# V of batches 1 and 2 loaded in token rows, and k of batches 3 to 7 in token rows and transposed by DMA out of SBUF

## The chip, the cores and the metric

The kernel runs on one core of a Trainium2 chip. The metric is the device time of one execution in microseconds; the median of the runs of the kernel before is 349.85 us.

## The reference

Eight batches of eight heads attend over 576 tokens of 64 numbers each, every query to itself and the 63 keys before it. The heads' outputs of a token stand side by side as 512 numbers and go through two matrix products with `h - tanh(h)` between them.

```python
B, H, S, D = 8, 8, 576, 64                        # q, k, v: float32
scores = matmul(q, k.transpose(0, 1, 3, 2)) / sqrt(D)
rel = pos[:, None] - pos[None, :]
scores = where((rel >= 0) & (rel < 64), scores, -1e9)
attn = exp(scores - max); attn = attn / (sum(attn) + 1e-9)
x = matmul(attn, v).transpose(0, 2, 1, 3).reshape(B * S, H * D)   # 4608 x 512
h = x @ w_in                                      # 512 x 2048
return (h - tanh(h)) @ w_out                      # 2048 x 512
```

## The kernel before

**The attention** works on a pair of heads at a time. Pair `pr` of batch `b` is heads `pr` and `pr + 4`, and `g = 4 b + pr` counts the 32 pairs. The tokens are cut into nine windows of 64 queries. For window `j` the scores need the 128 keys from 64 before the window to its end; so `kT`, in which a column is a key and the 128 partitions are the two heads' 64 numbers, has 64 columns of zeros in front. `scores` (L256 to L264) multiplies three windows at a time with `qT` and lets ScalarE take the exponential. `masking` clears what lies outside the 64 keys, `pv` (L270) multiplies with V, `norm` divides by the sum, which a column of ones in V has produced, and writes `xs`. The outputs get to the feature-major tile `xT` through TensorE (`x_tr`, first batches) or through an SP DMA that transposes (`x_dma`, from batch 2 on).

**V** has to lie with 128 keys on the partitions for each of nine windows, and neighbouring windows share 64 keys: `vw[b % 2]`, 128 partitions by nine windows by eight heads by 65 (64 numbers and the one). There are two ways to fill it:

- Batches 0 to 2: V is loaded whole with eight tokens in a row of a partition (`load_v_all`, 72 partitions), cast into the tile `vb` pair by pair (`cast_v`), copied by nine DMAs into the upper halves of the windows (`keys_v`, L162), and the upper halves are copied to the next window's lower halves (`shift_v`: for batches 0 and 1 by VectorE, L168, for batch 2 by one SP DMA, L170).
- Batches 3 to 7: five POOL DMAs put 128 tokens each onto the partitions of every other window (`load_rows`, L175), in rows of 64 numbers that the DMA converts to bf16, and `cross_rows` (L181, L182) makes the halves that are still missing, with two VectorE copies.

**q and k** are loaded whole for a batch with six tokens in a partition's row (`load_all`, 96 partitions), cast by POOL pair by pair (`cast`, L85), and turned by six TensorE transposes a pair into PSUM (`tr`, L247), from which ScalarE and VectorE copy them into `qT` and `kT` (L83, L85). In batch 7 both are bounced through DRAM instead: `bounce` writes the cast rows out, and an SP DMA reads them back transposed (`tr_dma`, L138 and L141).

**The two matrix products** run over nine chunks of 512 tokens and 16 blocks of the 2048 hidden numbers: `hp_mm` (L317), the tanh on ScalarE (L321), the subtraction on VectorE (L327), and 16 steps later `yp_mm` (L337), `y_out` (L342) and the store on SP's queue (L344).

**The order** is written out by hand (`manual_schedule`). A loop counts half steps `h`; an even one issues the four matmuls of one block of the first product, an odd one four of the second. `items[h]` holds what else is issued at `h`. For the first twelve pairs that comes from the text `PLAN`, one token a call; what stands under -1 comes ahead of the first product. `V1` and `V2` are the loads of V of batches 1 and 2, `d..` casts, `k..` the copies to `vw`, `z..` the shifts, `K`, `Q` whole loads, `w0` to `w2` and `o0` to `o3` the weights. For pairs 12 to 31 a loop sets the places by formula: with `d` = 0, 2 or 4, the scores of pair `g` start at `a + 5`, `a = 8 g - 48 - d`, and loads are placed from the batch's mark `s = 32 b - d`. `pace` is a tiny POOL copy that reads a fresh hidden block, so that POOL doesn't issue a load too early:

```python
s = 32 * b - (0, 2, 4)[min(b - 3, 2)]
...
    for i in range(NF + 1):
        at(s - 59 + i, load_rows, b, i)
    at(s - 42, cross_rows, b)
...
        hq, hk = s - (60 if b < 7 else 68), s - (64 if b < 7 else 72)
```

Each engine takes its instructions in the order in which the loop issues them, so that one that waits holds what is behind it. Loads with conversion are issued by POOL, transposing DMAs and stores by SP.

Of the kernel before, what the change touches and what calls it, by code (L numbers as in the profile page):

```python
# [8 lines left out]
BF16 = mybir.dt.bfloat16  # L9
# [6 lines left out]
def kernel(  # L16
# [9 lines left out]
    nc = tc.nc  # L26
    B, H, S, D = q.shape
    NP = H // 2
    NJ = S // 64
    E, P = 6, S // 6  # L30
    EV, PV = 8, S // 8
# [40 lines left out]
    vb = const.tile([PV, EV, H, D + 1], BF16, name="vb")  # L72
    PT = [const.tile([128, NJ, 128], BF16, name=f"pt{i}") for i in range(NPT)]
    kT = [const.tile([128, 64 + S], BF16, name=f"kt{i}") for i in range(NR)]
    qT = [const.tile([128, 2, S], BF16, name=f"qt{i}") for i in range(NR)]
    qz = [const.tile([P, 2, E, 128], BF16, name=f"qz{i}") for i in range(2)]
    xs = [const.tile([128, NJ, NP, D], BF16, name=f"xs{i}") for i in range(2)]
# [9 lines left out]
    def load(g, n, eng):  # L87

        b, pr = divmod(g, NP)
        if eng is nc.gpsimd:  # L90
            if (b, n) not in whole:
                whole[b, n] = all_pool.tile([P, H, E * D], BF16, tag=n, name=n + "all")
            t = whole[b, n][:, pr::NP]
        else:
            t = qk_pool.tile([P, 2, E * D], F32, tag="f", name=n + "f")
        eng.dma_start(out=t, in_=(q if n == "q" else k)[b, pr::NP].rearrange("h (p e) d -> p h (e d)", e=E))
        stage[g, n] = t

    def load_all(b, n):

        t = all_pool.tile([P, H, E * D], BF16, tag=n, name=n + "all")
        nc.gpsimd.dma_start(out=t, in_=(q if n == "q" else k)[b].rearrange("h (p e) d -> p h (e d)", e=E))
        for pr in range(NP):
            stage[b * NP + pr, n] = t[:, pr::NP]
# [15 lines left out]
        for h in range(2):  # L120
            nc.gpsimd.tensor_copy(qz[g % 2][:, h, :, 64 * h:64 * h + 64], i[:, h])

    def bounce(g, n):

        if n == "q":
            t = dram.tile([2, S, 128], BF16, tag="q", name="qd")
            nc.sync.dma_start(out=t.rearrange("h (p e) c -> p h (e c)", e=E),
                              in_=qz[g % 2].rearrange("p h e c -> p h (e c)"))
        else:
            t = dram.tile([S, 128], BF16, tag="k", name="kd")  # L130
            nc.sync.dma_start(out=t.rearrange("(p e) c -> p (e c)", e=E),
                              in_=rows.pop((g, "k")).rearrange("p e h d -> p (e h d)"))
        rows[g, n + "d"] = t

    def tr_dma(g, n):
        t = rows.pop((g, n + "d"))
        if n == "q":
            nc.sync.dma_start(out=qT[g % NR].rearrange("c h s -> c (h s)"),  # L138
                              in_=t.rearrange("h s c -> (h s) c"), transpose=True)
        else:  # L140
            nc.sync.dma_start(out=kT[g % NR][:, 64:], in_=t, transpose=True)  # L141

    def load_v(b, pr):
        if (b, "v") not in whole:
# [1 line left out]
        t = whole[b, "v"][:, pr::NP]  # L146
        nc.gpsimd.dma_start(out=t, in_=v[b, pr::NP].rearrange("h (p e) d -> p h (e d)", e=EV))
        stage[b, pr, "v"] = t

    def load_v_all(b):  # L150
        t = v_pool.tile([PV, H, EV * D], BF16, tag="v", name="vall")
        nc.gpsimd.dma_start(out=t, in_=v[b].rearrange("h (p e) d -> p h (e d)", e=EV))
        for pr in range(NP):
            stage[b, pr, "v"] = t[:, pr::NP]

    def cast_v(b, pr, eng=nc.gpsimd):
        move(eng, vb[:, :, 2 * pr:2 * pr + 2, 0:D].rearrange("p e h d -> p h e d"),
# [4 lines left out]
        eng.dma_start(out=vw[b % 2][64:128, j].rearrange("p h c -> p (h c)"),  # L162
                      in_=vb[8 * j:8 * j + 8].rearrange("p e h c -> p e (h c)"))

    def shift_v(b, j0, j1, eng=nc.sync):
        lo, hi = vw[b % 2][0:64, j0 + 1:j1 + 1], vw[b % 2][64:128, j0:j1]
        if eng is nc.vector:
            eng.tensor_copy(lo, hi)  # L168
        else:
            eng.dma_start(out=lo.rearrange("p j h c -> p (j h c)"), in_=hi.rearrange("p j h c -> p (j h c)"))  # L170

    def load_rows(b, i):

# [4 lines left out]
    def cross_rows(b):  # L178

        w = vw[b % 2]  # L180
        nc.vector.tensor_copy(w[0:64, 2::2], w[64:128, 1::2])  # L181
        nc.vector.tensor_copy(w[64:128, 0:NJ - 1:2], w[0:64, 1::2])  # L182

    w_in_r = moe_w_in.rearrange("(ko ki) f -> ki ko f", ki=128)

# [23 lines left out]
    def more_constants():  # L209
        nc.vector.memset(qT[1], 0.0)  # L210
        nc.vector.memset(kT[1][:, 0:64], 0.0)
        for i in range(2):
            nc.vector.memset(vw[i][0:64, 0], 0.0)

        for h in range(2):
            nc.gpsimd.memset(hide[:, h], 0.0)
            nc.gpsimd.affine_select(hide[:, h], hide[:, h], compare_op=ALU.is_ge, fill=-(2.0 ** 30),
                                    base=-1, pattern=[[-1, 64]], channel_multiplier=1)  # L220
            nc.gpsimd.affine_select(hide[:, h], hide[:, h], compare_op=ALU.is_ge, fill=-(2.0 ** 30),
                                    base=64, pattern=[[1, 64]], channel_multiplier=-1)
# [33 lines left out]
    def scores(g, grp, bank):  # L256
        sp = ps[:, bank, 0:384].rearrange("p (i q) -> p i q", i=3)
        for i in range(3):
            j = 3 * grp + i
            nc.tensor.matmul(sp[:, i, :], kT[g % NR][:, 64 * j:64 * j + 128],  # L260
                             qT[g % NR][:, :, 64 * j:64 * j + 64], start=True, stop=g >= 2 * NP)
            if g < 2 * NP:
                nc.tensor.matmul(sp[:, i, :], ident, hide.rearrange("p h t -> p (h t)"), start=False, stop=True)
        nc.scalar.activation(PT[g % NPT][:, 3 * grp:3 * grp + 3, :], sp, ACT.Exp, scale=scale)  # L264
# [5 lines left out]
    def pv(g, grp):  # L270
        b, pr = divmod(g, NP)
        for i in range(3):
            j = 3 * grp + i
            nc.tensor.matmul(ps[:, 5 + grp, 130 * i:130 * i + 130], PT[g % NPT][:, j, :],  # L274
                             vw[b % 2][:, j, pr::NP, :] if b > 2 else vw[b % 2][:, j, 2 * pr:2 * pr + 2, :], start=True, stop=True)

    def norm(g):
        b, pr = divmod(g, NP)
# [71 lines left out]
    def at(h, *fn):  # L350
        items.setdefault(h, []).append(fn)
# [14 lines left out]
    def play(script):  # L366
        for step in script.split():
# [5 lines left out]
            elif what in "QK":  # L373
                load_all(*n, what.lower())
            elif what == "V":
                load_v_all(*n)
            elif what == "a":
                cast(*n, "q", *eng)
            elif what == "b":
# [5 lines left out]
            elif what == "k":  # L385
                keys_v(*n, *eng)
            elif what == "z":
                for j in (0, 4) if eng[0] is nc.vector else (0,):
                    shift_v(*n, j, j + 4 if eng[0] is nc.vector else NJ - 1, *eng)
            elif what == "E":  # L390
                tr(*n, "q", 3, *eng)
            elif what == "F":
# [27 lines left out]
        -1: """  # L420
            r2a q0s v02 v03 v00 v01 a0v r0s d00a d01v d02a m i r1p q3p q1a d03p b0a k01s a1v
            k08s k00s b1p k03p n k02s F0a E0av R01 R02 q2p E1av k07p V1 k06a a3p k04p b2v K1 a2a
            R00 F1v k05s r3a E2aa F2a Q1 w0 R10 z0v d12p R22 d13p R12 P0 R11 E3aa R20 P1 d10p
            b3a d11p k12s k13p R21 k16p a7p w1 F3a b4a P2 a4p R30 R31 X000v Q2 R32 P3 b7a X001a
            k10s K2 b5p a6p F4a k18s w2 X010v k11s k17s b6p a5p b9p V2 k15a X011v E4vv""",
        0: "b8p",
        10: "R42 F5v k14s E5aa",
        12: "a8v R41 o2 o1 a9p d20p z1v",
        15: "R50 o3 R40 E6av F6v d21p R51 R52 E7aa P4 d22p R62 F7a R61 bAa o0 d23p P5 k25s R60",
        16: "E8aa k23p aAp R70",  # L430
        20: "R72 k20s X100v k27s X101a P6",
        23: "F8a R71 F9a k21p k22p aBp R80 P7 E9av k26s bBp k24p R82",
        24: "R81 X111v k28s X110a R91",
        31: "R90 z2s EAav M8",
        32: "R92",
        35: "FAa",
        36: "RA1 M9",
# [13 lines left out]
    for g in range(3 * NP, B * NP):  # L451
        b, pr = divmod(g, NP)
        a = 8 * g - 48 - (0, 2, 4)[min(b - 3, 2)]
        s = 32 * b - (0, 2, 4)[min(b - 3, 2)]
        if b < 7:
            at(a - 7, cast, g, "q")
            at(a, tr, g, "q", 3, nc.scalar, nc.vector)
        else:
            at(a - 14, cast_q, g)
            at(a - 12, bounce, g, "q")  # L460
            at(a - 6, tr_dma, g, "q")
        if b < 7:
            at(a - 5, cast, g, "k")
            at(a + 2, tr, g, "k", 3, nc.scalar)
        else:
            at(a - 13, cast, g, "k")
            at(a - 11, bounce, g, "k")
            at(a - 5, tr_dma, g, "k")
        for i in range(3):
            at(a + 5 + 2 * i, scores, g, i, 4)  # L470
        at(a + 11, masking, g)
        for i in range(3):
            at(a + 13 + i, pv, g, i)
        at(a + 15, norm, g)
        if pr == NP - 1:
            at(a + 16, x_dma, b)
        if pr == 0:
            for i in range(NF + 1):
                at(s - 59 + i, load_rows, b, i)
            at(s - 42, cross_rows, b)  # L480
        if pr == 0:
            if b < 4:
                at(s - 64, load_all, b, "q")
                at(s - 63, load_all, b, "k")
            else:
                hq, hk = s - (60 if b < 7 else 68), s - (64 if b < 7 else 72)
                for h, f in (hq, (load_all, b, "q")), (hk, (load_all, b, "k")):
                    at(h, pace, h)
                    at(h, *f)

    LAG = 16
    for h in range(min(items), 2 * (16 * NC + LAG) + 2):
# [43 lines left out]
```

## Time and profile before

| | us |
|---|---|
| runs | 353.31, 349.85, 349.43; median 349.85 |
| profiled execution | 354.17 |
| its span, first to last instruction | 352.4 |
| PE busy | 314.9 |
| VectorE, ScalarE, POOL busy | 205.0, 192.8, 107.9 |
| first matmul of the first product (L317) | starts at 39.6 |

The busy times of the engines overlap. The time of the profiled execution is a little more than its span, since something lies before the first and after the last instruction. The page's rows with 40 digits cut the span into slices of 8.8 us. In a row of the timeline, the first number is the start, the second the length, both in us from the start of the span, and a bracket at the end gives how long the engine had stood idle and for whom.

### The profile page before, as it was taken

How to read it: one execution, taken by the hardware profiler on the slowest of the kernel's cores; microseconds unless marked ns; L12 is line 12 of the kernel's file. 1: busy time of each engine (PE TensorE's matmuls, PEld its weight loads, DVE VectorE, ACT ScalarE, POOL GpSimd, SP SyncE). 2: the span in 40 equal slices, each digit the busy share in tenths (PEclk: the TensorE clock that was granted, in tenths of full speed). 3: DMA queues.
4: the chain of work that ended last, by engine and by line, in shares of the span. 5: the costliest groups of instructions: out<-in, count | busy, mean ns of one | idle time of the engine just before them, and what ended most of it. 6: DMA issues, size and time to landing. Idle time of an engine off the chain costs nothing.

```text
span 352.4 us, 5650 instructions
## 1 busy us (share of the span) xinstructions
PE 314.9 (89%) x2142; PEld 180.1 (51%) x2173; DVE 205.0 (58%) x324; ACT 192.8 (55%) x347; POOL 107.9 (31%) x156
## 2 busy tenths in 40 slices
PE   0277778897899999999999999999999999999995
PEld 0266456554555555555555555555555444444442
DVE  1335776863777668766867686676666433333300
ACT  1466578863565666566666666655554444444421
POOL 7728623953203760265034342810000000000000
PEclk9999999998999999999999999999999999999999
DMA  8699999999204990893099469986601400010012
GB/s 172 122 160 186 162 190 173 172 145 180 38 32 74 165 91 34 158 156 46 30 163 156 72 79 198 140 198 132 175 32 38 119 32 30 30 61 30 30 71 80
DMA packets 70315, 38.31 MB, mean 109 GB/s; under 512 B 47104, under 2 KB 64448, under 8 KB 70224
## 3 DMA queue, kind: packets, MB, share of 16 engines
q0 software_dynamic: 40032, 18.22, 46.4%
q1 hardware_dynamic: 29488, 18.71, 20.1%
q10 hardware_dynamic: 768, 1.02, 1.0%
q8 instruction: 17, 0.28, 0.3%
q14 instruction: 10, 0.08, 0.1%
HBM read 36.70 MB, written 11.21 MB: 136 GB/s over the span
## 4 chain that ended last, share of the span: by engine, by line
PE 69%; DMA 15%; POOL 6%; DVE 4%; issue 3%; ACT 2%; ACTq 0%; POOLq 0%; SPq 0%; DVEq 0%
PE ps L337 32%; PE ps L317 28%; DMA vall<-in_v_dram 5%; DMA vw<-vb 4%; DMA kall<-in_k_dram 4%; PE ps L274 4%; PE ps L260 3%; DMA vw<-vw 3%; PE ps L247 2%; POOL vb L85 2%; DVE xs L285 1%; POOL vw L162 1%; DVE gT L327 1%; POOL qb L85 1%; ACT th L321 1%
## 5 line engine op out<-in xcount | busy, mean ns | idle before, releaser
L327 DVE TENSOR_TENSOR gT<-ps,th 128x512 bf16<-128x512 f32 x144 | 99.2, 691 | 87.4 <-ACT th L321 84.2
L317 PE MATMUL ps<-xT,wi 128*128 128x512 bf16 x576 | 148.0, 381 | 1.8 <-DVE gT L327 1.7
L337 PE MATMUL ps<-w_out_sb,gT 128*128 128x512 bf16 x545 | 140.3, 379 | 1.8 <-ACT ysb L342 0.2
L321 ACT ACTIVATE th<-ps 128x512 f32<-128x512 f32 x144 | 85.9, 597 | 80.3 <-PE ps L317 80.1
L317 PEld LDWEIGHTS <-wi 128*128 128x128 bf16 x576 | 61.1, 113 | 47.8 <-issue 3.6
L337 PEld LDWEIGHTS <-gT 128*128 128x128 bf16 x576 | 54.0, 97 | 56.1 <-issue 0.9
L264 ACT ACTIVATE pt<-ps 128x384 bf16<-128x384 f32 x96 | 46.9, 489 | 45.0 <-PE ps L260 37.5
L285 DVE TENSOR_TENSOR xs<-ps,rc 64x576 bf16<-64x576 f32 x64 | 48.3, 755 | 1.5
L260 PE MATMUL ps<-qt,kt 128*128 128x128 bf16 x288 | 36.9, 228 | 6.3 <-ACT pt L264 3.8
L274 PE MATMUL ps<-vw,pt 128*128 128x130 bf16 x288 | 30.3, 228 | 6.1 <-DMA vw<-vw 2.3
L274 PEld LDWEIGHTS <-pt 128*128 128x128 bf16 x288 | 23.0, 101 | 22.5 <-issue 3.2
L342 ACT ACTIVATE ysb<-ps 128x512 f32<-128x512 f32 x36 | 21.5, 596 | 16.0 <-PE ps L337 16.0
L260 PEld LDWEIGHTS <-kt 128*128 128x128 bf16 x288 | 24.6, 102 | 9.8 <-ACT kt L83 1.9
L85 DVE COPY qt<-ps 64x576 bf16<-64x576 bf16 x24 | 18.2, 758 | 17.3 <-ACT qt L83 17.2
L85 POOL COPY qb<-qall 96x768 bf16<-96x768 bf16 x24 | 20.0, 833 | 20.6 <-DMA qall<-in_q_dram 18.3
L85 POOL COPY kb<-kall 96x768 bf16<-96x768 bf16 x26 | 21.6, 833 | 12.2 <-DMA kall<-in_k_dram 11.9
L83 ACT ACTIVATE qt<-ps 64x576 bf16<-64x576 bf16 x32 | 20.4, 636 | 1.4 <-PE ps L247 1.2
L175 POOL DMA_DIRECT2D vw<-in_v_dram x25 | 21.1, 860 | 0.0
L109 POOL COPY tick<-gT 1x1 bf16<-1x1 bf16 x8 | 1.4, 180 | 62.9 <-DVE gT L327 55.3
L83 ACT ACTIVATE kt<-ps 128x576 bf16<-128x576 bf16 x25 | 16.2, 648 | 4.3 <-PE ps L247 4.2
L268 DVE TENSOR_TENSOR pt<-pt,ps 128x1152 bf16<-128x1152 bf16 x24 | 17.9, 744 | 0.0
L247 PE MATMUL ps<-ident,kb 96*128 96x96 bf16 x168 | 12.8, 217 | 2.0 <-ACT xT L83 0.9
(55 smaller groups left out, 144.9 us busy)
## 6 DMA issues: line engine op xcount, KB each, us to landing
out_dram<-ysb SPq DMA_DIRECT2D x36, 256.0 KB
kall<-in_k_dram POOLq DMA_DIRECT2D x7, 576.0 KB, 6.8
qall<-in_q_dram POOLq DMA_DIRECT2D x7, 576.0 KB, 9.1
vw<-in_v_dram POOLq DMA_DIRECT2D x20, 128.0 KB, 8.3
w_out_sb<-in_moe_w_out_dram POOLq DMA_DIRECT2D x4, 512.0 KB, 8.6
vall<-in_v_dram POOLq DMA_DIRECT2D x2, 576.0 KB, 10.4
qd<-qz SPq DMA_DIRECT2D x4, 288.0 KB
vw<-vb SPq DMA_DIRECT2D x16, 65.0 KB
```

Source lines behind the costliest of these rows:

```text
L83: nc.scalar.activation(o, i, ACT.Copy)
L85: eng.tensor_copy(o, i)
L175: nc.gpsimd.dma_start(out=w[:, 2 * i + 1, :, 0:D] if i < NF else w[64:128, 2 * i, :, 0:D], in_=v[b, :, 128 * i:128 * i + n].rearrange("h p ...
L260: nc.tensor.matmul(sp[:, i, :], kT[g % NR][:, 64 * j:64 * j + 128], qT[g % NR][:, :, 64 * j:64 * j + 64], start=True, stop=g >= 2 * NP)
L264: nc.scalar.activation(PT[g % NPT][:, 3 * grp:3 * grp + 3, :], sp, ACT.Exp, scale=scale)
L274: nc.tensor.matmul(ps[:, 5 + grp, 130 * i:130 * i + 130], PT[g % NPT][:, j, :], vw[b % 2][:, j, pr::NP, :] if b > 2 else vw[b % 2][:, j, 2 ...
L285: nc.vector.tensor_tensor(xo[r, :, :, pr, :], ov[r, :, :, h, 0:D], rc[r].to_broadcast([64, 3, 3, 64]), ALU.mult)
L317: nc.tensor.matmul(hp, w_in_tile(ki, m), chunk_tile(c)[:, :, ki % 2, 64 * (ki // 2):64 * (ki // 2) + 64], start=(ki == 0), stop=(ki == 3))
L321: nc.scalar.activation(th, hp, ACT.Tanh)
L327: nc.vector.tensor_tensor(gT[c][:, m, :], hp, th, ALU.subtract)
L337: nc.tensor.matmul(yp, gT[c][:, m, s * 128:(s + 1) * 128], w_out_sb[:, m, :], start=(m == 0), stop=(m == M - 1))
L342: nc.scalar.activation(ysb, ps[:, yp_bank(c, s), :], ACT.Copy)
```

## The change

V: batches 1 and 2 take the second way, `load_rows` and `cross_rows`; `load_v_all`, their casts, their copies through `vb` and the SP form of `shift_v` go. `vw[1]` needs its column of ones from a memset, since nothing copies it there any more.

k: for batches 3 to 7 a new `load_k` puts 128 tokens of all eight heads onto the partitions, in ten POOL DMAs a batch (five pieces by two halves of the heads), and a new `tr_k` transposes each piece for all four pairs at once by an SP DMA from SBUF into the new tile `kw[b % 2]`, from which the scores read. The whole load of k, its casts, its TensorE transposes and copies (batches 3 to 6) and its way through DRAM (batch 7) go.

The places of the loads in the loop move: V rows from `s - 59` to `s - 68`, q from `s - 60` (batch 3: `s - 64`; batch 7: `s - 68`) to `s - 62` (batch 7: `s - 69`), paced for batch 3 too, k from `s - 64` (batch 3: `s - 63`; batch 7: `s - 72`) to `s - 61` through `s - 53`.

```diff
+    kw = [const.tile([128, NP, 64 + S], BF16, name=f"kw{i}") for i in range(2)]
...
+    def load_k(b, i):
+        if i == 0:
+            t = all_pool.tile([128, H, E * D], BF16, tag="k", name="kall")
+            t = t.rearrange("p h f -> p (h f)")[:, 0:(NF + 1) * H * D]
+            whole[b, "k"] = t.rearrange("p (i r h d) -> p i r h d", r=NP, h=2, d=D)
+        c = min(128, S - 128 * i)
+        src = k[b, :, 128 * i:128 * i + c].rearrange("(h r) p d -> p h r d", h=2)
+        for h in range(2):
+            nc.gpsimd.dma_start(out=whole[b, "k"][0:c, i, :, h, :], in_=src[:, h])
+
+    def tr_k(b, i):
+        c = min(128, S - 128 * i)
+        nc.sync.dma_start(out=kw[b % 2][:, :, 64 + 128 * i:64 + 128 * i + c],
+                          in_=whole[b, "k"][0:c, i].rearrange("p r h d -> p (r h d)"), transpose=True)
...
+            nc.vector.memset(kw[i][:, :, 0:64], 0.0)
+            if i == 1:
+                nc.vector.memset(vw[i][:, :, :, D], 1.0)
...
-            nc.tensor.matmul(sp[:, i, :], kT[g % NR][:, 64 * j:64 * j + 128],
+            kt = kT[g % NR] if g < 3 * NP else kw[g // NP % 2][:, g % NP]
+            nc.tensor.matmul(sp[:, i, :], kt[:, 64 * j:64 * j + 128],
...
             elif what == "V":
-                load_v_all(*n)
+                for i in range(NF + 1):
+                    load_rows(*n, i)
...
             elif what == "z":
-                for j in (0, 4) if eng[0] is nc.vector else (0,):
-                    shift_v(*n, j, j + 4 if eng[0] is nc.vector else NJ - 1, *eng)
+                if n[0] > 0:
+                    cross_rows(*n)
+                for j in (0, 4) if n[0] == 0 else ():
+                    shift_v(*n, j, j + 4)
...
             for i in range(NF + 1):
-                at(s - 59 + i, load_rows, b, i)
+                at(s - 68 + i, load_rows, b, i)
+                at(s - 61 + 2 * i, load_k, b, i)
+                at(s - 51 + i, tr_k, b, i)
             at(s - 42, cross_rows, b)
...
+            hq = s - (62 if b < 7 else 69)
+            at(hq, pace, hq)
+            at(hq, load_all, b, "q")
```

In `PLAN` the tokens `d1.`, `d2.`, `k1.` and `k2.` go, `z1v` becomes `z1` and `z2s` becomes `z2`; the rest keeps its order.

More of the change, by code (lines that the diff above doesn't have):

```diff
@@ L91, in load @@
             if (b, n) not in whole:
-                whole[b, n] = all_pool.tile([P, H, E * D], BF16, tag=n, name=n + "all")
+                whole[b, n] = all_pool.tile([128, H, E * D], BF16, tag=n, name=n + "all")[0:P]
             t = whole[b, n][:, pr::NP]
@@ L99, in load_all @@
     def load_all(b, n):
-        t = all_pool.tile([P, H, E * D], BF16, tag=n, name=n + "all")
+        t = all_pool.tile([128, H, E * D], BF16, tag=n, name=n + "all")[0:P]
         nc.gpsimd.dma_start(out=t, in_=(q if n == "q" else k)[b].rearrange("h (p e) d -> p h (e d)", e=E))
@@ L121, in cast_q, with bounce, tr_dma @@
             nc.gpsimd.tensor_copy(qz[g % 2][:, h, :, 64 * h:64 * h + 64], i[:, h])
[L123 to L141, printed above, removed]
+    def bounce(g):
+        t = dram.tile([2, S, 128], BF16, tag="q", name="qd")
+        nc.sync.dma_start(out=t.rearrange("h (p e) c -> p h (e c)", e=E),
+                          in_=qz[g % 2].rearrange("p h e c -> p h (e c)"))
+        rows[g, "qd"] = t
+    def tr_dma(g):
+        nc.sync.dma_start(out=qT[g % NR].rearrange("c h s -> c (h s)"),
+                          in_=rows.pop((g, "qd")).rearrange("h s c -> (h s) c"), transpose=True)
     def load_v(b, pr):
@@ L148, in load_v @@
         stage[b, pr, "v"] = t
[L150 to L154, printed above, removed]
     def cast_v(b, pr, eng=nc.gpsimd):
@@ L163, in keys_v, with shift_v @@
                       in_=vb[8 * j:8 * j + 8].rearrange("p e h c -> p e (h c)"))
[L165 to L170, printed above, removed]
+    def shift_v(b, j0, j1):
+        nc.vector.tensor_copy(vw[b % 2][0:64, j0 + 1:j1 + 1], vw[b % 2][64:128, j0:j1])
     def load_rows(b, i):
@@ L274, in pv @@
             nc.tensor.matmul(ps[:, 5 + grp, 130 * i:130 * i + 130], PT[g % NPT][:, j, :],
-                             vw[b % 2][:, j, pr::NP, :] if b > 2 else vw[b % 2][:, j, 2 * pr:2 * pr + 2, :], start=True, stop=True)
+                             vw[b % 2][:, j, pr::NP, :] if b > 0 else vw[b % 2][:, j, 2 * pr:2 * pr + 2, :], start=True, stop=True)
     def norm(g):
@@ L422 @@
             k08s k00s b1p k03p n k02s F0a E0av R01 R02 q2p E1av k07p V1 k06a a3p k04p b2v K1 a2a
-            R00 F1v k05s r3a E2aa F2a Q1 w0 R10 z0v d12p R22 d13p R12 P0 R11 E3aa R20 P1 d10p
-            b3a d11p k12s k13p R21 k16p a7p w1 F3a b4a P2 a4p R30 R31 X000v Q2 R32 P3 b7a X001a
-            k10s K2 b5p a6p F4a k18s w2 X010v k11s k17s b6p a5p b9p V2 k15a X011v E4vv""",
+            R00 F1v k05s r3a E2aa F2a Q1 w0 R10 z0v R22 R12 P0 R11 E3aa R20 P1
+            b3a R21 a7p w1 F3a b4a P2 a4p R30 R31 X000v Q2 R32 P3 b7a X001a
+            K2 b5p a6p F4a w2 X010v b6p a5p b9p V2 X011v E4vv""",
         0: "b8p",
[L427 to L434, printed above, removed]
+        10: "R42 F5v E5aa",
+        12: "a8v R41 o2 o1 a9p z1",
+        15: "R50 o3 R40 E6av F6v R51 R52 E7aa P4 R62 F7a R61 bAa o0 P5 R60",
+        16: "E8aa aAp R70",
+        20: "R72 X100v X101a P6",
+        23: "F8a R71 F9a aBp R80 P7 E9av bBp R82",
+        24: "R81 X111v X110a R91",
+        31: "R90 z2 EAav M8",
         32: "R92",
@@ L459 @@
             at(a - 14, cast_q, g)
[L460 to L468, printed above, removed]
+            at(a - 12, bounce, g)
+            at(a - 6, tr_dma, g)
         for i in range(3):
@@ L478 @@
             for i in range(NF + 1):
-                at(s - 59 + i, load_rows, b, i)
+                at(s - 68 + i, load_rows, b, i)
+                at(s - 61 + 2 * i, load_k, b, i)
+                at(s - 51 + i, tr_k, b, i)
             at(s - 42, cross_rows, b)
         if pr == 0:
[L482 to L489, printed above, removed]
+            hq = s - (62 if b < 7 else 69)
+            at(hq, pace, hq)
+            at(hq, load_all, b, "q")
     LAG = 16
```

## The prediction

> **What bounds the kernel now.** I read the page first, then the chain, the waits, the timeline of TensorE around each wait, and last the DMA queues with the times to landing.
>
> ```profile
> span 352.4 us, 5650 instructions
> PE 314.9 (89%) x2142; PEld 180.1 (51%) x2173; DVE 205.0 (58%) x324; ACT 192.8 (55%) x347; POOL 107.9 (31%) x156
> ...
> PE   0277778897899999999999999999999999999995
> ...
> PEclk9999999998999999999999999999999999999999
> DMA  8699999999204990893099469986601400010012
> ```
>
> PE stands at nine tenths from the twelfth slice (about 97 us) to the end; no other engine is near it. The windows say it more sharply: from 200 to 260 us PE is busy 59.62 of 60 us, from 140 to 200 us 58.56. From about 100 us on, the time is therefore the sum of PE's work, and each microsecond that PE doesn't spend comes off the end. Ahead of that lies a start in which PE waits, and the DMA engines are busy nearly throughout.
>
> The waits show one place ahead of 100 us where PE stands for long once it has become dense:
>
> ```profile
> 80.59 1.03 PE L337 MATMUL ps<-w_out_sb,gT 128*128 128x512 bf16 x4
> 81.46 0.22 PE L274 MATMUL ps<-vw,pt 128*128 128x130 bf16 x1
> 83.99 1.05 PE L274 MATMUL ps<-vw,pt 128*128 128x130 bf16 x8 [2.32 <-DMA vw<-vw]
> 84.84 0.53 PE L260 MATMUL ps<-qt,kt 128*128 128x128 bf16 x3
> ```
>
> The product with V of batch 2's pair 1 has begun, and its other eight matmuls stand 2.32 us for the one SP DMA that copies V's halves across (`z2s`, L170). The window from 83.7 to 87.1 us then has a granted clock of 0.50, where its neighbours have 1.00: half of 3.4 us, 1.7 us of work, is lost as well. The Trainium skill (TensorE: Matmul & The Clock Gate, Part 1) says that an idle window of some 3.4 us brings the half clock. The row agrees in length, though the idle time that brought it was only 2.3 us.
>
> The chain ahead of that copy runs over work that the change deletes (load of V as a whole, POOL's casts, the copies through `vb`):
>
> ```profile
> 50.97 9.40 DMA vall<-in_v_dram
> 61.94 2.04 POOL vb L85 x2
> 64.44 1.09 POOL vb L85
> 69.83 4.09 DMA vw<-vb
> 74.11 9.84 DMA vw<-vw
> ```
>
> **Part 1, k transposed by DMA.** For batches 3 to 6, sixteen pairs, each with six TensorE transposes, go. Here is one group and its successor:
>
> ```profile
> 75.80 0.42 PE L247 MATMUL ps<-ident,kb 96*128 96x96 bf16 x6
> 76.06 1.03 PE L317 MATMUL ps<-xT,wi 128*128 128x512 bf16 x4
> ```
>
> From start to start a group holds PE 0.26 us: 16 x 0.26 = **4.2 us off PE**. The page's group (168 in 12.8 us, 76 ns each) would give 96 x 76 ns = 7.3 us, but its busy time counts the end of each group that overlaps the next instruction. I take 4.2 and keep 7.3 as the upper bound. Batch 7 had its k by DMA already and gives PE nothing. ACT loses 16 copies of 0.65 us and POOL 20 casts of 0.83 us; neither engine ends a wait of PE there, so this counts nothing. One PE wait of 0.39 us at 107.4 us, of a k transpose for its PSUM bank, goes too: with the 0.2 us that PE's weight load waits for `wi`, when eight copies through `vb` no longer run beside that load, **0.4 us**, taken with some trust (0 to 0.6).
>
> What it adds: ten POOL issues per batch. The nearest row is V's last piece, also 512 rows of 128 bytes:
>
> ```profile
> L175 POOL DMA_DIRECT2D vw<-in_v_dram x25: 690/893/936, 72.0 to 223.9; - x25
> DMA to landing us min/median/max: 3.8/7.3/15.9
> ```
>
> Eight of 0.69 us and two shorter ones, about 6.8 us per batch against 0.78 + 4 x 0.83 = 4.1 us removed; POOL is busy 31%, so it is hidden. Behind them on POOL stands the cast of q. With the order of the steps, pieces 3 and 4 of k come after the cast of the batch's first q, which waits for q to land, and that is the price to follow.
>
> The transfer is the larger matter. A batch of k now comes in 768 packets of 768 bytes; in rows it takes 4608 of 128, as V does. Counted in the trace's packet records, V's rows average 40 ns on an engine: 4608 / 16 x 40 ns = 11.5 us if an engine does one at a time, against 768 / 16 x 91 ns = 4.4 us. But packets overlap. Between 84 and 88 us 3011 of them went, between 156 and 160 us 3491: some 700 per us, hence 6.6 us for a batch. For batch 5, q and V together went from an issue at 150.12 to the last landing at 162.81, 12.7 us. That is 1.5 times the 4.4 us of the larger packets, not 2.6 times. The Trainium skill (DMA: Bandwidth & Descriptors, Specifications) speaks against this part: writes below 512 bytes don't run at line rate and become read-modify-write. As an estimate from that rule, rows would take at least twice the 4.4 us, so V and k of a batch some 4.4 us longer together than by the 6.6, and the sum would come to as much as 355 us instead of the 343 below.
>
> So per batch, in half steps h of 1.04 us (a batch is 32 of them and takes 33.3 us, between the transposes at 141.8 and 175.1 us), counted back from the batch's mark s: V is issued from s-68 (it may start some earlier, when the product with V of two batches before is done, at s-73), and its data pass in 6.6 us. q is issued at s-62 and needs about 5 us, three pieces of k follow at once with 4.4 us, and q lands near s-55. Then the cast, and pieces 3 and 4, out by s-52, landed by about s-48 (3.8 us at least from issue to landing). The SP transposes: 2304 packets of 256 bytes, which the same number for x crosses in under 4 us (176 to 180 us), issues of 1.2 us; the last is down near s-45. The scores ask for the first pieces at s-43 and for the last at s-39. That leaves 2 to 6 us, so I take **0**; the bounds are 0 and 4 us in each of five batches. On SP the transposes wait for k's landings, and the stores of y stand behind them: a store per 8 h, with three buffers, so 24 h of cover. If the cover goes, ACT's copy and then PE wait.
>
> **Part 2, V of batches 1 and 2 in rows.** Off go two whole loads, 8 casts of 1.11 us, 16 copies through `vb` and the SP copy. What waits is now `cross_rows`, two DVE copies of 0.70 us; for batch 1 they replace two of the same length, for batch 2 DVE gets 1.4 us more at h = 31, near 72 us, under PE's work (DVE is busy 12.11 of the 16 us from 60 to 76; 1.4 us if that cover is gone). V of batch 2 is issued from about 50 us, as before, by five issues to 54 us, and at 15.9 us, the worst landing in the row above, is there by 70 us, before the copy is due. So **2.3 + 1.7 = 4.0 us** go. Bounds: 0 if these waits aren't in a usual run, 4.0 if they are.
>
> Part 2 also moves load on POOL's queue at the start: the five issues of batch 1's V, 4 x 0.88 + 0.70 = 4.2 us instead of 0.84, stand ahead of `k04p`, K1, Q1 and `w0`, 3.4 us later on POOL. Behind `k04p` is the first product with V:
>
> ```profile
> 16.82 10.27 DMA vw<-vb
> ```
>
> That copy takes 10.27 us and lands 0.4 us after V of batch 1 does (26.71), because it is queued behind it. In rows, V moves in 6.6 us from about 17.5 and would land near 26 again, and so would the copy, issued at 20.2 us. On the other hand POOL no longer waits 7.6 us for `vb` at 19.7 us, nor casts for 4.5 us, so `w1`, Q2 and K2 don't come later. I take **0**, between -1 (landed sooner) and +3.4 (the delay of the issue comes through whole). The new constants are three memsets on DVE near 11 us, some tenths of a us, where it then idles 0.60 us for q: nothing.
>
> **The sum.** 4.2 + 4.0 + 0.4 = 8.6 us off the profiled execution, whose own time is 354.17 us (span 352.4, the rest before and after): 345.6. The median of the runs is 349.85, 4.3 us shorter, so a part of the stall at 82 us may be missing from it; which, nothing shows. I count half of the 4.0: 349.85 - 4.2 - 2.0 - 0.4 = **343.2 us**. About 1%, 3.5 us, is what a measurement of this kernel can tell from no change.
>
> **Rivals.**
>
> *The stall isn't in a usual run* (0.15): only the transposes and the 0.4 count, 345.2 us. For it: runs of 349.43 and 349.85 beside 353.31. Against it: the chain runs through the copy for 33 us.
>
> *k comes late* (0.17, slower). Place: the first scores of each batch from 3 to 7. If the rows don't overlap on the engines, because SP's transposes and stores share them, V, q and k need 11.5 + 4.4 + 11.5 = 27.4 us instead of some 18; 9 us later less some 5 of margin is 4 us in five batches, 20 us: 343.2 + 20 = 363. It decides from 6.6 / 5 = 1.3 us per batch. For it: the page's DMA row at 9 in many slices; a landing of 15.9 us at 74 us. Against it: the slices of 2, 0, 3 between loads, and 162.81 above.
>
> *The start comes later* (0.12): the 3.4 us on POOL's queue pass to PE, 343.2 + 3.4 = 346.6. For it, `k04p` is on the chain; against it, its landing is set by V's data.
>
> *PE isn't what the transposes took time from* (0.06): the freed 4.2 us become waits for ACT and DVE, 347.9 with half of the stall. Against it, 59.62 of 60.
>
> **How the numbers follow.** The forecast has 0.50, with 340 to 345. Faster by over 1% (below 346.35): it and the first rival, with a little off the others, 0.67. Within 1%: the start and PE, 0.16. Slower: late k, 0.17. The lower end is 341.2 with all of the stall, and 3.1 more off for transposes at the page's price: 338. The upper end takes in the start's delay and late k of up to 1.8 us per batch: 352.
>
> **What would show it.** Right: 96 fewer TensorE transposes (L247 on `kb` 72 instead of 168), no wait of PE for V near 80 us, no clock of 0.50 there, PE at nine tenths after; `kw` in none of PE's waits. Part 1 wrong: PE waiting for a DMA into `kw` at each batch's first scores, with POOL's cast of q later than now. Part 2 wrong: the first L317 later than 39.6 us, or DVE waiting for V at h = 31. The forecast falls if PE's idle time after 100 us grows by over 4 us.

## The result, and the profile after

The changed kernel is **slower**: a median of 354.37 us over 20 runs against 351.05 for the kernel before in as many, a ratio of 1.0066 (95% interval 1.0044 to 1.0088). The ratio goes by the fast runs alone, without two of the changed kernel that lie far above its fastest, and is not the quotient of the two medians, which is 1.0095. The forecast was 343.2 with a range of 338 to 352. In ten later runs on another occasion the changed kernel had 355.16 (ratio 1.0084, 1.005 to 1.0119).

The profiled execution of the changed kernel is one of its best: 350.95 us where eleven of its 20 runs take 354 and more. That matters for the reading, so a second profile of the same kernel stands beside it below.

From the page of the changed kernel, the rows that answer to those of before:

```profile
span 349.2 us, 5466 instructions
PE 309.6 (89%) x2047; PEld 175.3 (50%) x2077; DVE 207.5 (59%) x329; ACT 184.1 (53%) x331; POOL 119.8 (34%) x172
...
PE   0277788889896999999999999999999999999995
...
PEclk9999999999999999999999999999999999999999
DMA  8699999949639955994989949988201400110021
```

The 7 in the tenth slice (79 to 88 us), where PE stood for V, is now a 9, but there is a 6 in the thirteenth slice that wasn't there. The wait of the product with V near 82 us is gone (first row of the timeline). The transposes of k are 72 where there were 168 (the view of the tile `kb`, before and after). A new wait has come (last row of the timeline):

```profile
81.91 0.69 PE L276 MATMUL ps<-vw,pt 128*128 128x130 bf16 x9
...
108.43 0.33 PE L262 MATMUL ps<-qt,kw 128*128 128x128 bf16 x3
111.84 1.05 PE L319 MATMUL ps<-xT,wi 128*128 128x512 bf16 x4 [3.09 <-DMA xT<-xs]
```

```profile
L247 PE MATMUL ps<-ident,kb x168: 202/206/287, 14.2 to 224.7; 96*128 96x96 bf16 x168
...
L248 PE MATMUL ps<-ident,kb x72: 202/206/288, 14.1 to 82.8; 96*128 96x96 bf16 x72
```

The wait is that of the first product (L319, L317 before) of chunk 2 at step 32, for `x_dma` of batch 2, which turns that batch's outputs. In the kernel before, the same product starts without a wait, and the loads of V of batch 4 come after it:

```profile
106.65 3.20 SPq L306 DMA_TRANSPOSE xT<-xs  x2
...
112.78 1.03 PE L317 MATMUL ps<-xT,wi 128*128 128x512 bf16 x4
...
118.66 0.88 POOL L175 DMA_DIRECT2D vw<-in_v_dram  x1
```

In the changed kernel POOL and SP in the same stretch, and the landing times of the tile `xT`, show what differs:

```profile
101.45 4.22 POOL L157 DMA_DIRECT2D vw<-in_v_dram  x5 [13.06 <-PE ps L248]
102.88 4.42 SPq L308 DMA_TRANSPOSE xT<-xs  x2
```

```profile
DMA to landing us min/median/max: 2.5/2.8/8.9
```

V of batch 4 is now issued at h = 58, the very place of `x_dma`, and 1.4 us ahead of it; in the kernel before it came at h = 67. The first transposing DMA of batch 2 lands after 8.9 us, and its reader stands six half steps, some 6 us, behind it. Of the other eleven the trace records two landings, after 2.5 and 2.8 us; with V of batch 4 moved back (experiments below) the same DMA takes 3.8 us. V of batch 5 and `x_dma` of batch 3 share a place too, h = 88, and PE doesn't wait there: V is issued 5.2 us ahead (135.08 and 140.24 us), and the reader stands eight half steps behind.

In the second profile of the changed kernel (span 352.4 us), the wait is 3.45 us and is followed by what the first was spared. In this windows view the columns are the length, the busy time of PE, PEld, DVE, ACT and POOL (with the number of instructions), the granted clock, the DMA share, which passes 1 where packets are in flight side by side, and GB/s:

```profile
110.00:113.40 3.40, 0.03 (x1) 0.03 (x2) 1.58 (x3) 0.94 (x2) 3.01 (x5) 1.00 2.35 103
113.40:116.80 3.40, 3.40 (x13) 1.48 (x14) 0.34 (x1) 1.12 (x2) 3.40 (x5) 0.51 1.29 211
```

PE stands for the whole of the first 3.4 us, and the next 3.4 us, one window of half clock, cost another 1.7 us. The mean granted clock of a run, where it is recorded, tells how often, though not where: half of 3.4 in some 350 us makes 0.995 one such window, and 0.99 two. At 0.99 or less are 21 of 30 runs of the changed kernel, and 15 of 54 of the kernel before. At the full clock (0.998 or more) are 3 of 30, with 350.46 to 351.32 us, and 12 of 54, with 349.13 to 351.91. The clock isn't the whole spread: the 18 runs of before at 0.995 reach from 349.78 to 355.44.

To see where time comes and goes, here is the start of the first product at chosen steps in four profiles, in us from the start of the span (read from the trace: the first of each four matmuls into `ps` from `xT`; h is twice the step):

| step | before | before, second profile | changed | changed, second |
|---|---|---|---|---|
| 0 | 39.63 | 39.06 | 39.22 | 39.41 |
| 16 | 72.18 | 71.61 | 71.81 | 72.97 |
| 18 | 76.06 | 75.49 | 76.57 | 77.74 |
| 20 | 79.73 | 79.16 | 80.19 | 81.36 |
| 22 | 88.10 | 83.55 | 84.59 | 85.76 |
| 30 | 108.47 | 103.92 | 104.28 | 105.45 |
| 32 | 112.78 | 108.24 | 111.84 | 113.37 |
| 34 | 117.02 | 112.48 | 115.75 | 118.95 |
| 88 | 233.49 | 228.95 | 230.04 | 233.24 |
| 143 | 333.10 | 328.55 | 329.64 | 332.84 |

From 20 to 22 the first profile of before loses 4.0 us to its wait for V; the second has nothing of it. From 16 to 18 the changed kernel loses 0.9 us. From 30 to 32 it loses 3.2 and 3.6, and 1.3 more to step 34 in the second profile. From 34 to 88 it gains 2.2 us, and in the first profile 0.7 from 22 to 30 and 0.3 from 32 to 34: 3.2 in all, where the transposes went. At step 143 the two profiles with no half clock on the way, before's second and the changed kernel's first, lie 1.1 us apart.

### The profile page after: what moved, and what is told of

Its sections match the earlier page's. It is cut to its first block, busy times and chain, and to the rows that moved or that the text cites. A ratio compares the mean times of both kernels' runs of the same rounds, so it can differ in the third digit from the quotient of the medians.

```text
span 349.2 us, 5466 instructions
## 1 busy us (share of the span) xinstructions
PE 309.6 (89%) x2047; PEld 175.3 (50%) x2077; DVE 207.5 (59%) x329; ACT 184.1 (53%) x331; POOL 119.8 (34%) x172
## 4 chain that ended last, share of the span: by engine, by line
PE 73%; DVE 8%; DMA 6%; ACT 5%; issue 3%; POOL 3%; ACTq 0%; DVEq 0%; POOLq 0%
PE ps L339 32%; PE ps L319 31%; PE ps L276 5%; PE ps L262 4%; DVE xs L287 3%; DMA xT<-xs 3%; DMA vw<-vb 2%; DMA vall<-in_v_dram 2%; DVE gT L329 2%; ACT th L323 2%; PE ps L248 1%; DVE qt L86 1%; POOL vw L157 1%; ACT pt L266 1%; ACT qt L84 1%
## 5 line engine op out<-in xcount | busy, mean ns | idle before, releaser
L319 PE MATMUL ps<-xT,wi 128*128 128x512 bf16 x576 | 147.3, 379 | 5.9 <-DMA xT<-xs 3.1
L319 PEld LDWEIGHTS <-wi 128*128 128x128 bf16 x576 | 60.9, 113 | 51.9 <-issue 4.4
L157 POOL DMA_DIRECT2D vw<-in_v_dram x35 | 30.1, 876 | 38.4 <-PE ps L262 23.4
L175 POOL DMA_DIRECT2D kall<-in_k_dram x50 | 36.1, 746 | 1.4 <-DMA vw<-in_v_dram 1.1
L262 PE MATMUL ps<-qt,kt 128*128 128x128 bf16 x108 | 16.9, 241 | 6.3 <-ACT pt L266 3.8
L262 PE MATMUL ps<-qt,kw 128*128 128x128 bf16 x180 | 19.7, 218 | 0.0
L262 PEld LDWEIGHTS <-kw 128*128 128x128 bf16 x180 | 13.5, 96 | 5.2
L248 PE MATMUL ps<-ident,qb 96*128 96x96 bf16 x168 | 12.8, 216 | 1.1 <-ACT qb L84 1.1
L262 PEld LDWEIGHTS <-kt 128*128 128x128 bf16 x108 | 11.1, 109 | 4.4 <-ACT kt L84 1.5
```

What stands on the lines that cost most here:

```text
L157: nc.gpsimd.dma_start(out=w[:, 2 * i + 1, :, 0:D] if i < NF else w[64:128, 2 * i, :, 0:D], in_=v[b, :, 128 * i:128 * i + n].rearrange("h p ...
L175: nc.gpsimd.dma_start(out=whole[b, "k"][0:c, i, :, h, :], in_=src[:, h])
L262: nc.tensor.matmul(sp[:, i, :], kt[:, 64 * j:64 * j + 128], qT[g % NR][:, :, 64 * j:64 * j + 64], start=True, stop=g >= 2 * NP)
L319: nc.tensor.matmul(hp, w_in_tile(ki, m), chunk_tile(c)[:, :, ki % 2, 64 * (ki // 2):64 * (ki // 2) + 64], start=(ki == 0), stop=(ki == 3))
```

## The experiments

Theory A: the loss is the meeting of V of batch 4 with the transposing DMA, and the half clock behind it. B: the start is later. C: k is late. Of each edit only the lines that differ from the kernel named are shown. A name in quotes after a heading is what later expectations call that run.

**The changed kernel once more** (no edit).

> The changed kernel unedited, for a second profile. Theory A (the loss is PE's wait for the transposing DMA into xT of batch 2, 3.1 us in the first profile, and the half clock that follows it): 353 to 355 us; the wait on xT again, 3 us or more, and one or two windows of half clock right behind it, which the first profile (350.95 us) was lucky not to have. Theory B (the start is later, by V of batch 1 on POOL's queue): no half clock, and a first L319 later than 40 us. Theory C (k late): PE waits for a DMA into kw.

Measured 355.16 us, just above A's 353 to 355, with the wait of 3.45 us and the half clock shown above, one window of it. B's sign, a late step 0 with a full clock, isn't there (39.41), nor is a wait for `kw`. Another window of half clock, at 38.3 us, lies in the start and has nothing to do with `xT`.

**V of batches 4 to 7 where it was** ("v_late", against the changed kernel).

```diff
-                at(s - 68 + i, load_rows, b, i)
+                at(s - (68 if b == 3 else 59) + i, load_rows, b, i)
```

> The changed kernel with V's rows of batches 4 to 7 issued at s - 59, as before the change, instead of s - 68, so that V of batch 4 no longer goes on the DMA engines together with the transposing DMA of batch 2's outputs. Theory A: the wait on xT falls from 3.1 us to under 0.5, the half clock goes, and the time falls by 4 to 7 us, to 347 to 350. Theory B and C: no change, 353 to 355; C could even be worse by 1 to 3 us, since k then shares the engines with V.

Measured 350.06 us, ratio to before 0.9936 (0.9903 to 0.9969): 5.1 us under the changed kernel, which ran on the same chip. The wait on `xT` is gone: step 32 comes 4.3 us after step 30, where the changed kernel takes 7.6, and `x_dma` lands after 3.8 us. The half clock behind that wait is gone with it, but this profile has 17 us of half clock in the start (23.2 to 36.8 and 40.2 to 43.6 us), so A's "the half clock goes" holds for that one place. A holds, with the time at the upper end of its 347 to 350; the place of V turned a gain of 0.6% into a loss.

**The meeting alone, in the kernel before.**

```diff
-                at(s - 59 + i, load_rows, b, i)
+                at(s - (68 if b == 4 else 59) + i, load_rows, b, i)
```

> The kernel before with one place changed: V's rows of batch 4 are issued at s - 68 instead of s - 59, beside the transposing DMA of batch 2's outputs; k and V of batches 1 and 2 are as before. If that meeting alone makes PE's wait on xT (theory A): a wait of 2 to 4 us on xT near 110 us, half clock in many runs, and 353 to 357, 2 to 5 us slower than before. If k's own DMAs are needed for it (theory C): 350 to 353, as before, and no wait on xT.

Measured 356.0 us, ratio 1.0114 (1.0052 to 1.0177). Its profile has the wait without any of k's new DMAs, and, 30 us ahead of it, the old one for V:

```profile
84.86 0.63 PE L274 MATMUL ps<-vw,pt 128*128 128x130 bf16 x8 [3.08 <-DMA vw<-vw]
...
104.88 0.89 POOL L175 DMA_DIRECT2D vw<-in_v_dram  x1 [13.62 <-PE ps L247]
...
106.03 4.10 SPq L306 DMA_TRANSPOSE xT<-xs  x2
...
114.47 1.05 PE L317 MATMUL ps<-xT,wi 128*128 128x512 bf16 x4 [2.16 <-DMA xT<-xs]
```

The half clock follows neither wait in this profile. So moving those five loads is enough to make the wait of 2.16 us, and moving them back removes it (above together with those of batches 5 to 7, further down without them). The time of 356.0 holds the old wait for V as well, so the 1.1% isn't the price of `xT` alone. That the loads and the transposing DMA hinder each other on the DMA engines is the reading; what in the engines slows the transposing one wasn't taken apart.

**Each part alone.** The V part in the kernel before, with the loads from batch 3 on as before:

> The kernel before with the V part alone (batches 1 and 2 in rows); k and all loads from batch 3 on are as before. Theory A: 347 to 351, at most the 4.0 us of the wait near 82 us gained, and no wait on xT. Theory B: 352 to 354, slower than before. Theory C says nothing against 347.

Measured 351.64 us, ratio 1.0008 (0.9972 to 1.0043): the V part is worth nothing that can be told from no change. The median lies between A's 351 and B's 352 and doesn't tell them apart. Its profile has no wait for V. Against the second profile of before, which has none either, it is 0.3 us late at step 16 (71.91), loses 0.9 more up to step 18 (76.68 against 75.49) and nothing after. That is what the part costs where there is no wait to remove.

The k part, with the changed places, and V of batches 1 and 2 as before:

> The changed kernel with V of batches 1 and 2 as before the change (whole loads, casts, copies through vb); k and the places of all loads from batch 3 on are the changed ones. Theory A: 352 to 357, the wait on xT is there, and the wait for V near 82 us too. Theory B: 346 to 348, since the start is as before and 4.2 us of transposes are off. Theory C: 353 to 357 with PE waiting for kw.

Measured 351.35 us, ratio 0.999 (0.9941 to 1.0039), just under A's 352 to 357, with the wait on `xT` of 2.31 us as A says. But A's other sign, the wait for V near 82 us, is not there: a miss. The reason stays open. The SP copy of V, issued at 71.44 us, has loads beside it here too: V of batch 3 is issued from 68.12 us on, ahead of it, and has landed by 79.76; what moved behind it are the loads of q and k (from 73.70 us, where the first profile of before issues them from 70.38, ahead of its copy at 74.11). Then the k part with V of batches 4 to 7 at the old place ("k_late"):

> The k part alone (V of batches 1 and 2 as before the change) and V's rows of batches 4 to 7 at s - 59. Theory A: k's part by itself is worth 3.2 us (16 groups of transposes of 0.26 us, less five waits of 0.2 us for the output copy), so 347.5 to 349.5 and a ratio of 0.988 to 0.993. Theory C: k in rows costs what it saves, ratio 0.996 to 1.004.

Measured 347.57 us, ratio 0.9891 (0.9833 to 0.9949), a gain of some 3.8 us. From step 22 to 88 its profile takes 142.2 us (82.66 to 224.89), the second profile of before 145.4 (83.55 to 228.95): 3.2 us gained, as A says.

**Is the wait for V of before in every run?**

> The kernel before, unedited, for a second profile. Theory D (the wait for V near 82 us is in nearly every run of before, 2.3 us with a half clock behind it): the wait is there again, 2 us or more. Theory E (the first profile had an unusually long one, which is why its 354.17 lies above the median): the wait is under 1 us, and no half clock follows it.

It isn't: 349.6 us, a span of 347.9, and no such wait. E holds here and D doesn't. But two of the three profiles in which V of batch 2 and the loads of batch 3 stand as before have the wait (2.32 and 3.08 us, the second with no half clock behind it), so it comes and goes. How many runs have it, and so its price in a median, isn't measured.

**The VectorE copies of batch 2 at h = 37** ("late_z2", against the changed kernel, with V of batches 4 to 7 at the old place).

```diff
-        31: "R90 z2 EAav M8",
+        31: "R90 EAav M8",
...
+        37: "z2",
```

> The changed kernel with V's rows of batches 4 to 7 at s - 59, and with the two VectorE copies that complete V of batch 2 issued at h = 37 instead of 31. In the table of steps, the changed kernel loses 0.9 us against before between steps 16 and 18, where these copies stand ahead of the subtractions. Theory F (that loss is theirs): step 18 starts 4.6 to 5.0 us after step 16 less 0.7, and the time is 0.7 to 1 us under that of v_late (350.06), 349 to 349.5. Rival: the copies are late for the product at h = 41, and the loss comes back there: 350 or more.

In the changed kernel, the copies stand ahead of the subtraction that frees the PSUM bank of the first product (timeline, VectorE and PE):

```profile
72.93 0.70 DVE L163 COPY vw<-vw 64x2080 bf16<-64x2080 bf16 x1
...
73.64 0.70 DVE L164 COPY vw<-vw 64x2080 bf16<-64x2080 bf16 x1
74.37 0.76 DVE L86 COPY qt<-ps 64x576 bf16<-64x576 bf16 x1
75.16 0.75 DVE L270 TENSOR_TENSOR pt<-pt,ps 128x1152 bf16<-128x1152 bf16 x1
75.83 1.28 DVE L329 TENSOR_TENSOR gT<-ps,th 128x512 bf16<-128x512 f32 x2
...
76.57 1.02 PE L319 MATMUL ps<-xT,wi 128*128 128x512 bf16 x4 [0.72 <-DVE gT L329]
```

At 37 the loss from step 16 to 18 is gone: 3.88 us between them (71.14 to 75.02), as before, against 4.76, a little under F's 3.9 to 4.3. The time was 349.35 us, within F's 349 to 349.5, but the ratio to before, taken on another occasion than v_late's, is the same 0.9936 (0.9895 to 0.9977), so the times don't show the gain. A part of it is lost again: this profile takes 1.6 us more than before between steps 88 and 94:

```profile
228.69 0.45 PE L262 MATMUL ps<-qt,kw 128*128 128x128 bf16 x3 [1.28 <-DMA kw<-kall]
```

Here theory C has its one place: at the first scores of batch 7, when V of batch 7 is issued at the old place, after q and among the pieces of k, k comes late. The wait there is 1.28 us in this profile, 0.36 in that of k_late and 0.08 in that of v_late, and none in those with V of batch 7 at the new place.

**Only V of batch 4 moved back, and the copies at 37** ("late4_z2").

```diff
-                at(s - 68 + i, load_rows, b, i)
+                at(s - (59 if b == 4 else 68) + i, load_rows, b, i)
...
+        37: "z2",
```

> The changed kernel with V's rows at s - 59 for batch 4 alone (batches 5 to 7 stay at s - 68) and the copies for V of batch 2 at h = 37. In late_z2, where V of all four batches was moved, PE waited 1.3 us for kw at the first scores of batch 7, with V and k on the engines together. Theory A with that: no wait on xT, none for kw, 347 to 349.5, a ratio of 0.988 to 0.993. Theory C in full: the waits for kw stay, 349 to 351.

Measured 348.34 us, ratio 0.9892 (0.9838 to 0.9947), with neither wait. One batch's five loads are what turned the sign; the copies at 37, which this kernel has too, account for at most the 0.9 us of steps 16 to 18.

**And V of batch 1 issued after `w0`.**

```diff
-            ... E1av k07p V1 k06a a3p k04p b2v K1 a2a
-            R00 F1v k05s r3a E2aa F2a Q1 w0 R10 z0v R22 ...
+            ... E1av k07p k06a a3p k04p b2v K1 a2a
+            R00 F1v k05s r3a E2aa F2a Q1 w0 V1 R10 z0v R22 ...
```

> As late4_z2, and V of batch 1 issued after w0 instead of ahead of k04p. In five profiles with V of batch 1 in rows the DMA of k04p lands at 26.6 us on average, in five with the whole load at 25.7, and the first product with V waits for it. Theory G (V's rows in front hold that copy): it lands by 22 us, the first L319 starts 0.5 to 1.7 us earlier than the 38.6 to 40.7 of the kernels with rows, and the time is that much below late4_z2. Rival (the chain of ScalarE and VectorE sets the start): the copy lands early and L319 still starts at 39 us or later.

Measured **345.5 us**, ratio to before 0.9835 (0.9789 to 0.9881), the best of all; with the three edits together the changed kernel is 1.2 to 2.1% faster than the kernel before. The copy `k04p` lands at 19.33 us instead of 27.52, and VectorE's second shift of batch 0's V, which waits for copies through `vb`, runs at 25.43 instead of 27.60. First the kernel without this edit (late4_z2), then with it:

```profile
27.60 0.70 DVE L152 COPY vw<-vw 64x2080 bf16<-64x2080 bf16 x1 [4.72 <-DMA vw<-vb]
...
40.46 2.81 PE L319 MATMUL ps<-xT,wi 128*128 128x512 bf16 x8
```

```profile
25.43 0.70 DVE L152 COPY vw<-vw 64x2080 bf16<-64x2080 bf16 x1 [2.87 <-DMA vw<-vb]
...
37.81 2.00 PE L319 MATMUL ps<-xT,wi 128*128 128x512 bf16 x8
```

The first product starts 2.65 us earlier; 0.83 of that is an earlier first matmul of the whole program (13.66 against 14.49 us), which has no tie to the edit, and a half clock from 38.9 to 42.3 us in the first profile, which the second hasn't, lies in that stretch too. G holds in kind: the copy lands by 22 us and the first product starts sooner. In size it was too low, since the median fell by 2.84 us and not by 0.5 to 1.7. Runs at the full clock differ by less, 346.63 and 346.67 us without the edit, 345.44 to 345.52 in four of the five with it; the rest goes with the clock, which is full in five of the six runs, against two of six. The wait doesn't fall all the way with `k04p`: another copy through `vb` ends it then, whose landing the trace doesn't record.

## Why the prediction was wrong

It said faster by 1.9%, and the kernel became slower by 0.7%. By its steps:

- **What bounds the kernel**: right. From 100 us on PE's own sum counts, and each us that PE stands in that stretch, 3.1 to 3.6 for `xT`, stays in the end.
- **Part 1, the step that failed.** The prediction followed V's rows from s-68 to their own landing, and put x's transposes beside them only as a price per packet. It never asked whose time V's new place takes: at h = 58 stands `x_dma` of batch 2, on SP's queue, six half steps ahead of its reader. The sum held no term for that; it is 3.1 to 3.6 us of wait, and in one of two profiles 1.7 us of half clock behind it. With V moved back the median falls by 5.1 us. The rival of late k looked for the meeting of rows with SP's transposes at the right engines, and at the wrong end: it was V that made x late, and not V and x that made k late. That the 355 us which the prediction estimated for rows at half the rate lies near the measured 354.37 is luck: it reckoned with rows that take twice as long and make k late, and no wait for `kw` is in either profile of the changed kernel.
- **4.2 us for the transposes, and 0.4**: mechanism right, size off. The 16 groups go, and so does the wait of 0.39 us of a k transpose, 4.6 us together; but 3.2 us is what is gained (step 22 to 88 in k_late and, without the wait for `xT`, in the changed kernel). PE now stands elsewhere, which the sum put at nothing: five times 0.2 us for the output copy on ScalarE, where before has one, and 0.5 us more in two places for VectorE (0.23 at step 30, 0.69 instead of 0.45 at 174.66 us). These are 1.3 us more, which leaves 3.3. One of the five:

```profile
129.85 1.02 PE L339 MATMUL ps<-w_out_sb,gT 128*128 128x512 bf16 x3 [0.20 <-ACT ysb L344]
```

- **k's transfer at 0**: right in the changed kernel, where PE never waits for `kw`; 0.1 to 1.3 us with V of batch 7 at the old place, in one batch of five. In the changed kernel the ten pieces of batch 5 are issued from 146.28 us on and have landed by 156.76. The rule on transfers under 512 bytes in the Trainium skill (DMA: Bandwidth & Descriptors, Specifications) shows in no wait of PE there; what the rows cost the DMA engines themselves no run takes apart.
- **4.0 us for the wait for V, counted half**: the wait is there in some runs and absent in others, so counting a part of it was sound in kind, though nothing showed that the part is a half. The whole V part came to nothing (1.0008); the next two terms are as large as the 2.0 us counted.
- **1.4 us on VectorE at h = 31 at 0**: wrong. The cover was taken from a busy share, 12.11 of 16 us; in the order of the queue the copies stand ahead of the subtraction that PE waits for. It cost 0.9 us, of the 1.4 that it named for a cover that is gone.
- **The start at 0, within -1 to 3.4**: in the range, perhaps on the costly side. `k04p` lands at 26.6 us on average with the rows (26.68, 26.59, 26.76, 26.85, 26.12) and 25.7 with the whole load (27.09, 25.05, 26.13, 24.5, 25.63). In the same profiles the first product starts at 39.4 us on average against 38.8, with single ones between 37.4 and 40.7, so a cost of less than 1 us isn't told from the spread. That V's place there matters for the end is shown by the last experiment.

With a wait for V in half of the runs (-2.0), the terms read -3.2 - 2.0 + 0.9 + 0.9 + 3.3 + 1.7 = +1.6 us, where 0.7% is 2.3 and the medians differ by 3.3. Of these the -3.2, the first 0.9 and the 3.3 are read from profiles; the -2.0, the start's 0.9 and a 1.7 in every run are assumed. The rest isn't settled; half clocks in the start, which come and go with both kernels, are as large.

## What to carry to other kernels

When a load is moved to an earlier place, list what its new neighbours on the DMA engines are for, and how long their readers can wait; here the load itself had time in plenty, and the transfer beside it had 6 us to its reader. A short wait of a dense PE is paid twice if a window of half clock follows, so count the reader's slack before the load's. Where work is called hidden on an engine, look at what stands behind it in that engine's order and not at the engine's share.

## What the hardware showed that was not expected

The same kernel spreads by 5 to 6 us from run to run (350.46 to 355.84 for the changed kernel, 349.13 to 355.44 for 53 of 54 runs of before), in part with the granted clock: the second profile of the changed kernel has half the clock from 38.3 to 41.8 us, where the first has none, and both start their first product within 0.2 us of each other. A wait of 3.09 us was followed by no half clock in one profile, one of 3.45 us by 3.4 us of it in the other, and one of 3.08 us (before with V of batch 4 moved) by none, while the one of 2.32 us in the first profile of before has half the clock from 83.7 us, just before its end, to 87.1. The stretches of half clock inside the spans last 3.4 us, 6.8 (late_z2) or 13.7 (v_late), whole multiples of one length. The Trainium skill (TensorE: Matmul & The Clock Gate, Part 1) says that the activity window runs free and doesn't reset when a kernel starts. By that it would be chance how a short wait falls into a window; these rows agree with it, but no run sets the phase.
